# Two attention units per stay of ScalarE's exponential table, with the gates' exponential in the same stay

## The chip, the cores and the metric

The kernel runs on one core of a Trainium2 chip. The core has five instruction streams that run side by side and meet only at semaphores: TensorE (PE in the profile, with its weight loads as PEld), VectorE (DVE), ScalarE (ACT), GpSimd (POOL) and SyncE (SP). Transfers are issued from SP, ACT and POOL queues and carried by 16 DMA engines. Each engine takes its own instructions strictly in the order in which the program lists them, so an instruction that waits holds up everything behind it on its engine.

The metric is the device time of one execution in microseconds. Three executions of the kernel before took 598.86, 600.32 and 600.51 us, median 600.32.

## What is computed

The inputs are 2048 tokens of 512 channels, in float32. Two branches are computed from the same tokens and mixed per token with a gate:

```
g = sigmoid((x * gate_w).sum(-1, keepdims=True))
# A: attention, 32 heads of 16 channels, each query sees 8 keys at distances 0, 2, ..., 14
logits = einsum("bhsd,bhswd->bhsw", q, kg) * 16 ** -0.5     # -1e9 before the first token
a = einsum("bhsw,bhswd->bhsd", softmax(logits), vg) @ wo
# B: gated feed-forward network, hidden width 1792
b = (gelu(x @ w_gate) * (x @ w_up)) @ w_down
return g * a + (1 - g) * b
```

The attention is too small for TensorE's array: eight keys per query. It is computed on VectorE, as elementwise products and reductions. TensorE does the projections and the feed-forward network, with each float32 operand split into a high and a low part (`hi`, `lo`) and three matmuls for a product: high by high, high by low, low by high.

## The kernel before, in words

**Halves, steps, units.** The tokens are worked off in two halves, `par` 0 and 1 (even and odd tokens, so that a distance of 2 is a distance of 1 within a half). For each half, `ffn(par)` runs 14 steps `f`, one for each 128 of the 1792 hidden channels. Between the two, `kq_second` computes keys and queries of the second half. The attention of a half is four **units** (`par`, `u`) of 128 channels, that is 8 heads.

**A step of the feed-forward network** (`gate_up`) makes the gate and up projections as seven block products of a Strassen-like scheme, called a11, s1, s2, a12, s4, s3, a22 after their token operands. Each is six matmuls of 128x512 on line L443 into one of the four PSUM banks `p`. In the profile, token operands show as `A` (a11, a12, a22) or `S` (s1, s2, s3, s4) and the weights as `g`; there are two weight tiles for a step, one with three operands (128x768, for a11, s1, s2) and one with four (128x1024, for the other four). ScalarE and VectorE empty the banks: L523 copies the product of a11 to a second bank, L448 copies twice to `s`, L538 and L554 are the GELUs (`c`), L453 adds, L457 multiplies gate by up, L459 and L460 split the result into `hh` and `hl`. The product a22 of a step is issued in the next step (`fourth`), and its GELU is L554.

**The weights of a step** are built ahead: VectorE forms sums (L382, three instructions a step), ScalarE writes the negated sum into the low part (L400), GpSimd adds the full sum onto it with an accumulating DMA (L401), and ScalarE writes the high part (L405). TensorE can begin a11 of a step only when the L401 transfer of its 128x768 tile has landed. In the second half the three-operand tile comes ready-made from HBM instead. The down projection (L486) runs in the same steps, two steps late; half of its sums are kept in SBUF and put back into a `p` bank by ScalarE before (L480) and taken out after (L502).

**A unit of the attention** is scores, softmax, gate, mix. `scores` is eight VectorE instructions of 2.3 us and a mask (L230). `softmax` is maximum (L237), subtraction (L239), exponential on ScalarE (L241), sum (L245) and reciprocal (L247). `gated` multiplies by the token's gate (L255, L257). `mix` multiplies by the values and adds up (L271 to L284). The gate itself needs one more exponential on ScalarE (L167, `gates`).

**What sets the order.** The program is not written engine by engine. The attention is a Python generator, and `pull` takes pieces of it between the products of a step; `LG`, `m` and the other tiles come from pools with one buffer, `lg` with two. A scheduler then orders each engine's instructions by priority and by when it reckons them ready, so a change at one place shifts rows on all engines for a long way behind it. `paced` ties an instruction to the matmul emitted last, `ordered` fixes the order of two instructions on an engine without a wait, and `after` makes one wait for another.

**ScalarE's tables.** Ahead of an activation whose function is not in the table that is loaded, the compiler puts an ACT_TABLE_LOAD. Plain copies appear behind either table without a load. Exponential (L241, L167) and GELU (L538, L554) do not share one, so each time that ScalarE goes to an exponential and back there are two loads. Such a visit is called a stay here.

Of the kernel before, what the change touches and what calls it, by code (L numbers as in the profile page):

```python
# [10 lines left out]
F32 = mybir.dt.float32  # L11
F32R = mybir.dt.float32r
AF = mybir.ActivationFunctionType
OP = mybir.AluOpType
AX = mybir.AxisListType

P = 128
S, D, F = 2048, 512, 1792
H, DH, W = 32, 16, 8
NT = S // P  # L20
NP = NT // 2
# [9 lines left out]
UH = UC // DH  # L31
# [17 lines left out]
def tile_gated_mix(ctx: ExitStack, tc: tile.TileContext, xt, wqkv, wff, wo, out):  # L49
    nc = tc.nc  # L50
    ctx.enter_context(nc.allow_non_contiguous_dma(reason="rows of 512 bytes"))
    pool = ctx.enter_context(tc.tile_pool(name="sb", bufs=1))
# [67 lines left out]
    z = pool.tile([P, 2, NP], F32, name="z")  # L120
# [42 lines left out]
        if not hh:  # L163
            nc.scalar.activation(z[:, par, jj:jj + 1], ps[:, CU:CU + 1], AF.Copy)

    def gates(par, ex=None):
        first = nc.scalar.activation(en, z[:, par], AF.Exp, scale=-1.0)  # L167
        if ex:
            ordered(first, ex)
        nc.vector.tensor_scalar_add(en, en, 1.0)  # L170
        nc.vector.reciprocal(g[:, par], en)
        nc.vector.tensor_scalar(gc[:, par], g[:, par], -1.0, 1.0, op0=OP.mult, op1=OP.add)
# [10 lines left out]
    LG = {}  # L183
# [8 lines left out]
    def load_kq(par, u):  # L192
        hh, c = divmod(u, 2)
        k, q = slots_of(u > 0), KQ["a"][:, 2 * NP - 1:]
        if u == 1:
            q = pool.tile([P, 2, BT * UC], F32, name="tb").rearrange("p a (b c) -> p (a b) c", c=UC)
        LG[par, u] = k, q
        if not u:
            return
        loads = load_slots(k, KS[par, hh][c])  # L200
        loads.append(nc.sync.dma_start(q, QS[par, hh][c].rearrange("(p j) d -> p j d", j=NP)))
        if not par and u < NU - 1:
            for ins in loads:
                after(ins, SCORED[-1])
# [13 lines left out]
    def scores(par, u):  # L218
# [12 lines left out]
            first, first, mask[:1, None, :NP - 1, :W - 1].to_broadcast([1, UH, NP - 1, W - 1]), op=OP.min)]  # L231
        LG[par, u] = lg

    def softmax(par, u):
        lg = LG[par, u]
        m = pool.tile([P, UH, NP], F32, name="m")
        nc.vector.tensor_reduce(m, lg, axis=AX.X, op=OP.max)  # L237
        yield 0.7
        nc.vector.tensor_tensor(lg, lg, m[:, :, :, None].to_broadcast([P, UH, NP, W]), op=OP.subtract)  # L239
        yield 0.7  # L240
        ex = nc.scalar.activation(lg, lg, AF.Exp, scale=DH ** -0.5)  # L241
        if not (par or u):
            ordered(ex, COPIED[-1])
            gates(par, ex)
        nc.vector.tensor_reduce(m, lg, axis=AX.X, op=OP.add)  # L245
        yield 0.7
        nc.vector.reciprocal(m, m)  # L247
        LG[par, u] = lg, m

    def gated(par, u):  # L250
        lg, m = LG[par, u]
        LG[par, u] = lg
        if par and not u:
            gates(par)
        nc.vector.tensor_tensor(m, m, g[:, par, None, :].to_broadcast([P, UH, NP]), op=OP.mult)  # L255
        yield 0.4
        nc.vector.tensor_tensor(lg, lg, m[:, :, :, None].to_broadcast([P, UH, NP, W]), op=OP.mult)  # L257
        yield 0.7
# [33 lines left out]
    def after(ins, other, cls=mybir.DependencyClass.Sync):  # L292

        tc.add_manual_dep(ins.ins, other.ins.name, mybir.DependencyInfo(cls, mybir.DependencyReason.SCHED_ONLY),
                          reason="pace")
# [4 lines left out]
    def ordered(ins, other):  # L300
        after(ins, other, mybir.DependencyClass.NoSync)

    def need(*key):
        while key not in done:
            yield None

    def attention():
        units = [(0, u) for u in range(NU)] + [(1, u) for u in range(NU)]
        yield from need(0, 0)
        load_kq(0, 0)  # L310
        yield from scores(0, 0)
        load_kq(0, 1)
        yield from scores(0, 1)
        yield from need(0, 1)
        scored, mixed = 2, False
        for i, un in enumerate(units):
            if scored == i:
                yield from need(un[0], un[1] // 2 * 2)
                load_kq(*un)
                if un[1]:  # L320
                    yield LOAD
                else:
                    load_kq(un[0], 1)
                yield from scores(*un)
                scored += 1
                mixed = False
            yield from softmax(*un)
            if un == (1, 0):
                yield from scores(*units[scored])
                scored += 1  # L330
                yield from need(un[0], 1)
            yield from gated(*un)


            to = units[scored] if scored < len(units) else None
            ahead = to and (to[0], to[1] // 2 * 2) in done
            if ahead:
                load_kq(*to)
            yield from mix(*un, LOAD if mixed else 0.0)
            done.add((*un, "o"))  # L340
            mixed = not ahead
            if ahead:
                yield from scores(*to)
                scored += 1

    fill = attention()
    credit = [0.0]

# [114 lines left out]
    late, COPIED = [], []  # L463
# [740 lines left out]
    en = pool.tile([P, NP], F32, name="en")  # L1204
# [51 lines left out]
```

## Time and profile before

| | |
|---|---|
| median of three runs | 600.32 us |
| the profiled execution's own time | 600.41 us |
| its span, first to last instruction | 598.5 us |
| TensorE matmuls busy | 591.7 us, 99% |
| TensorE weight loads busy | 493.0 us, 82% |
| VectorE busy | 529.3 us, 88% |
| ScalarE busy | 391.7 us, 65% |
| GpSimd busy | 89.2 us, 15% |
| ACT_TABLE_LOAD | 20, of 1283 ns each |
| TensorE clock granted | 1.000 |

The profile is of one execution. The 1.9 us between its span and its time lie outside the span. A row such as `L443 PE MATMUL p<-S,g 128*128 128x512 f32 x672 | 167.2, 389 | 0.0` is a group: line, engine, operation, tile written and tiles read, shapes, count, then busy microseconds of all, mean nanoseconds of one, idle microseconds of the engine just ahead of them and what ended that idle time. Durations of matmuls overlap, since they are pipelined, so the distance between starts tells more than their length. In a timeline the first two numbers are start and duration in microseconds, and a bracket at the end gives the idle time ahead of the row and what ended it.

### The profile page before, as it was taken

How to read it: one execution, taken by the hardware profiler on the slowest of the kernel's cores; microseconds unless marked ns; L12 is line 12 of the kernel's file. 1: busy time of each engine (PE TensorE's matmuls, PEld its weight loads, DVE VectorE, ACT ScalarE, POOL GpSimd, SP SyncE). 2: the span in 40 equal slices, each digit the busy share in tenths (PEclk: the TensorE clock that was granted, in tenths of full speed). 3: DMA queues.
4: the chain of work that ended last, by engine and by line, in shares of the span. 5: the costliest groups of instructions: out<-in, count | busy, mean ns of one | idle time of the engine just before them, and what ended most of it. 6: DMA issues, size and time to landing. Idle time of an engine off the chain costs nothing.

```text
span 598.5 us, 8195 instructions
## 1 busy us (share of the span) xinstructions
PE 591.7 (99%) x2778; PEld 493.0 (82%) x2778; DVE 529.3 (88%) x618; ACT 391.7 (65%) x670; POOL 89.2 (15%) x121
## 2 busy tenths in 40 slices
PE   8999999999999999999999999999999999999997
PEld 6889988878788888888788988888888888888886
DVE  5997979998996999799989988999998989799952
ACT  5846558686678767787772465677667656885532
POOL 0501011111111111102017000111111111101300
PEclk9999999999999999999999999999999999999999
DMA  8788897798989988978569948695967696737924
GB/s 312 268 245 249 234 321 199 173 291 220 268 253 237 245 260 231 295 235 328 199 196 317 285 141 281 152 254 125 276 164 229 174 276 159 226 107 193 144 53 156
DMA packets 80449, 134.18 MB, mean 224 GB/s; under 512 B 8092, under 2 KB 46362, under 8 KB 80152
## 3 DMA queue, kind: packets, MB, share of 16 engines
q1 hardware_dynamic: 62890, 97.67, 49.9%
q0 software_dynamic: 12576, 32.97, 28.0%
q10 hardware_dynamic: 4942, 3.01, 1.7%
q8 instruction: 22, 0.36, 0.3%
q14 instruction: 19, 0.16, 0.1%
HBM read 68.30 MB, written 38.86 MB: 179 GB/s over the span
## 4 chain that ended last, share of the span: by engine, by line
PE 90%; DMA 4%; issue 3%; DVE 1%; ACT 1%; SPq 0%; POOL 0%; POOLq 0%; ACTq 0%; DVEq 0%
PE p L443 41%; PE acc L486 11%; PE p L486 11%; PE acc L130 8%; PE acc L771 6%; PE p L771 6%; PE p L704 5%; DMA g<-raw 3%; PE acc L704 2%; DMA prod<-wqkv 1%; DVE g L771 0%; SPq L866 0%; DVE S L771 0%; DVE prod L275 0%; ACT rt L502 0%
## 5 line engine op out<-in xcount | busy, mean ns | idle before, releaser
L443 PE MATMUL p<-S,g 128*128 128x512 f32 x672 | 167.2, 389 | 0.0
L443 PEld LDWEIGHTS p<-S,g 128*128 128x128 f32 x672 | 125.7, 188 | 25.9
L443 PE MATMUL p<-A,g 128*128 128x512 f32 x504 | 128.8, 391 | 0.7 <-DMA g<-raw 0.7
L443 PEld LDWEIGHTS p<-A,g 128*128 128x128 f32 x504 | 93.9, 188 | 22.0 <-DMA g<-raw 1.5
L401 POOL DMA_DIRECT2D g<-raw x40 | 34.6, 865 | 271.1 <-ACT g L400 195.6
L226 DVE TENSOR_REDUCE lg<-prod 128x128 f32<-128x2048 f32 x32 | 72.9, 2278 | 0.1
L486 PE MATMUL p<-d,hh 128*128 128x512 f32 x224 | 68.4, 390 | 0.5 <-ACT p L480 0.5
L486 PE MATMUL acc<-d,hh 128*128 128x512 f32 x224 | 59.0, 390 | 0.0
L271 DVE TENSOR_TENSOR prod<-kq,lg 128x2048 f32<-128x2048 f32 x24 | 54.6, 2274 | 1.0 <-PE acc L486 0.7
L486 PEld LDWEIGHTS p<-d,hh 128*128 128x128 f32 x224 | 41.9, 188 | 9.8 <-ACT p L480 1.2
L486 PEld LDWEIGHTS acc<-d,hh 128*128 128x128 f32 x224 | 42.0, 188 | 8.9
L400 ACT ACTIVATE g<-raw 128x1024 fp32r<-128x1024 f32 (+1 forms) x40 | 39.4, 985 | 12.6 <-DVE raw L382 5.6
L405 ACT ACTIVATE g<-raw 128x1024 fp32r<-128x1024 f32 (+1 forms) x40 | 39.3, 986 | 11.7 <-PE p L443 11.7
L448 ACT ACTIVATE s<-p 128x512 f32<-128x512 f32 x56 | 33.1, 594 | 19.2 <-PE p L443 16.4
L453 DVE TENSOR_TENSOR c<-p,s 128x512 f32<-128x512 f32 x56 | 37.9, 680 | 8.3 <-PE p L443 7.4
L460 DVE TENSOR_TENSOR hl<-c,hh 128x512 fp32r<-128x512 f32 x56 | 38.2, 682 | 7.6 <-ACT hh L459 7.5
L457 DVE TENSOR_TENSOR c<-c 128x512 f32<-128x512 f32 x56 | 38.1, 681 | 6.4 <-ACT c L554 6.3
L459 ACT ACTIVATE hh<-c 128x512 fp32r<-128x512 f32 x56 | 35.1, 626 | 13.2 <-DVE c L457 13.0
L486 PE MATMUL p<-d,hl 128*128 128x512 f32 x112 | 42.4, 389 | 0.0
L502 ACT ACTIVATE rt<-p 128x512 f32<-128x512 f32 x48 | 28.1, 594 | 19.3 <-PE p L486 19.3
L275 DVE TENSOR_TENSOR prod<-prod 128x1024 f32<-128x1024 f32 x32 | 38.9, 1216 | 0.2
L130 PE MATMUL acc<-d,A 128*128 128x256 f32 (+1 forms) x288 | 37.9, 281 | 0.0
(183 smaller groups left out, 982.7 us busy)
## 6 DMA issues: line engine op xcount, KB each, us to landing
g<-raw POOLq DMA_DIRECT2D x27, 512.0 KB, 6.6
raw<-wff SPq DMA_DIRECT2D x42, 256.0 KB, 4.0
ws<-g SPq DMA_DIRECT2D x14, 768.0 KB, 5.8
g<-ws SPq DMA_DIRECT2D x14, 768.0 KB, 5.2
r<-wff SPq DMA_DIRECT2D x28, 256.0 KB, 5.0
d<-r POOLq DMA_DIRECT2D x24, 256.0 KB, 6.7
g<-raw POOLq DMA_DIRECT2D x13, 384.0 KB, 6.3
os<-tb SPq DMA_DIRECT2D x64, 64.0 KB, 3.4
```

The source lines that it names most:

```text
L130: LAST[:] = [nc.tensor.matmul(ps[:, :cn], a[:, t], w[:, c0:c0 + cn], start=(kc == 0 and n == 0), stop=(kc == KC - 1 and n == 2))]
L226: nc.vector.tensor_reduce(two_of(lg, jj), prod.rearrange("p j w (h d) -> p (j w) h d", d=DH), axis=AX.X, op=OP.add)
L271: paced(nc.vector.tensor_tensor(prod.rearrange("p j w (h d) -> p (j w) h d", d=DH), spans(v, jj).rearrange("p j w (h d) -> p j w h d", d=D ...
L275: nc.vector.tensor_tensor(prod[:, :, :4], prod[:, :, :4], prod[:, :, 4:], op=OP.add)
L400: nc.scalar.activation(lo, raw, AF.Copy, scale=-1.0)
L405: ins = nc.scalar.activation(hi, raw, AF.Copy)
L443: LAST[:] = [nc.tensor.matmul(ps, w_, a_, start=(start and kc == 0 and n == 0), stop=(kc == 1 and n == 2), skip_group_check=True)]
L457: nc.vector.tensor_tensor(ge, ge, up, op=OP.mult)
L460: nc.vector.tensor_tensor(hl_, ge, hh_.bitcast(F32), op=OP.subtract)
L486: ins = nc.tensor.matmul(pp, a[:, ts], w, start=(i == 0 and n == 0 and gr == 0), stop=(i == 1 and n == 2), skip_group_check=True)
L704: ins = nc.tensor.matmul(pa, a, b, start=(first and n == 0), stop=(last and n == 2), skip_group_check=True)
L771: return lambda *args, **kw: self.add(getattr(self.eng, name)(*args, **kw))
```

## The change

Before, each unit's softmax had its own exponential, and the gates' exponentials were one beside the first unit's and one by itself in the second half. That makes nine stays and, with the loads at the beginning, twenty table loads. After, `exps` is called at every even unit. It does maximum and subtraction of that unit and of the next, then both exponentials one behind the other; the first waits for the second unit's subtraction. At unit 0 of either half the gates' exponential follows at once. What remains in `softmax` is the sum and the reciprocal. At unit (1, 0) the scores of unit (1, 1) and the wait for the second half's values now stand ahead of the softmax, not inside it. There are four stays and ten table loads.

```diff
-    def gates(par, ex=None):
-        first = nc.scalar.activation(en, z[:, par], AF.Exp, scale=-1.0)
-        if ex:
-            ordered(first, ex)
+    def gates(par, ex):
+        ordered(nc.scalar.activation(en, z[:, par], AF.Exp, scale=-1.0), ex)
...
+    def exps(par, u):
+
+        for lg in (LG[par, u], LG[par, u + 1]):
+            m = pool.tile([P, UH, NP], F32, name="m")
+            nc.vector.tensor_reduce(m, lg, axis=AX.X, op=OP.max)
+            yield 0.7
+            sub = nc.vector.tensor_tensor(lg, lg, m[:, :, :, None].to_broadcast([P, UH, NP, W]), op=OP.subtract)
+            yield 0.7
+        for i in range(2):
+            lg = LG[par, u + i]
+            ex = nc.scalar.activation(lg, lg, AF.Exp, scale=DH ** -0.5)
+            if i:
+                ordered(ex, first)
+                continue
+            first = ex
+            after(ex, sub)
+            if not (par or u):
+                ordered(ex, COPIED[-1])
+        if not u:
+            gates(par, ex)
+
     def softmax(par, u):
+        if u % 2 == 0:
+            yield from exps(par, u)
         lg = LG[par, u]
         m = pool.tile([P, UH, NP], F32, name="m")
-        nc.vector.tensor_reduce(m, lg, axis=AX.X, op=OP.max)
-        yield 0.7
-        nc.vector.tensor_tensor(lg, lg, m[:, :, :, None].to_broadcast([P, UH, NP, W]), op=OP.subtract)
-        yield 0.7
-        ex = nc.scalar.activation(lg, lg, AF.Exp, scale=DH ** -0.5)
-        if not (par or u):
-            ordered(ex, COPIED[-1])
-            gates(par, ex)
         nc.vector.tensor_reduce(m, lg, axis=AX.X, op=OP.add)
...
     def gated(par, u):
...
-        if par and not u:
-            gates(par)
...
-            yield from softmax(*un)
             if un == (1, 0):
                 yield from scores(*units[scored])
                 scored += 1
                 yield from need(un[0], 1)
+            yield from softmax(*un)
             yield from gated(*un)
```

The scheduler's order of all engines differs from the first removed exponential on. In the changed kernel the lines behind the diff's first part lie lower: of those named here, L241 is L242, and the lines from L400 on are 11 higher (L400 is L411, L443 is L454, L523 is L534, L554 is L565), those of `softmax` and `gated` 13 and 11 (L245 is L258, L257 is L268). Three places matter.

**ScalarE, first half, around step 4.** Ahead of the step stood the exponential of unit (0, 0); this is where unit (0, 1)'s stood. L523 is the copy of step 4's a11. Before:

```order
L523 ACTIVATE p<-p 128x512
L459 ACTIVATE hh<-c 128x512
L448 ACTIVATE s<-p 128x512
L429 ACTIVATE d<-r 128x512
L448 ACTIVATE s<-p 128x512
L241 ACT_TABLE_LOAD
L241 ACTIVATE lg<-lg 128x512
L400 ACTIVATE g_1343<-raw 128x768
L405 ACTIVATE g_1343<-raw 128x768
L554 ACT_TABLE_LOAD
L554 ACTIVATE c<-p 128x512
L400 ACTIVATE g_1389<-raw 128x1024
```

After, from the last split ahead of the stay:

```order
L443 ACTIVATE d<-r 128x512
L242 ACT_TABLE_LOAD
L242 ACTIVATE lg<-lg 128x512 x2
L167 ACTIVATE en<-z 128x8
L470 ACTIVATE hh<-c 128x512
L513 ACTIVATE rt<-p 128x512
L534 ACTIVATE p<-p 128x512
L411 ACTIVATE g_1346<-raw 128x768
L565 ACT_TABLE_LOAD
L565 ACTIVATE c<-p 128x512
L411 ACTIVATE g_1393<-raw 128x1024
L491 ACTIVATE p<-rt 128x512
```

The stay with both units' exponentials and the gates' now stands ahead of L523 of step 4. The negated weights of step 5 (`g_1343` before, `g_1346` after) come right behind L523, and the load for the GELU comes behind them.

**TensorE and ScalarE, first half, from step 7 to step 8.** After the change, TensorE's rows between the second part of step 7 (`g_1664`) and a11 of step 8 (`g_1748`). Ahead of these twelve rows and behind a12 of step 7 stand another 9 down-projection matmuls:

```order
L497 MATMUL p<-d,hh 128x512 x2
L454 MATMUL p<-S,g_1664 128x512 x6
L497 MATMUL p<-d,hl 128x512
L454 MATMUL p<-S,g_1664 128x512 x6
L497 MATMUL acc_1071<-d,hl 128x512
L497 MATMUL acc_1072<-d,hl 128x512
L497 MATMUL acc_1073<-d,hl 128x512
L497 MATMUL p<-d,hh 128x512 x2
L497 MATMUL p<-d,hl 128x512
L497 MATMUL p<-d,hh 128x512 x2
L497 MATMUL p<-d,hl 128x512
L454 MATMUL p<-A,g_1748 128x512 x6
```

And ScalarE's rows of the same step, from the copy of a11 to the negated weights of step 8; L549 is the GELU of a12:

```order
L534 ACTIVATE p<-p 128x512
L565 ACTIVATE c<-p 128x512
L470 ACTIVATE hh<-c 128x512
L491 ACTIVATE p<-rt 128x512
L459 ACTIVATE s<-p 128x512 x2
L470 ACTIVATE hh<-c 128x512
L549 ACTIVATE c<-p 128x512
L411 ACTIVATE g_1748<-raw 128x768
L416 ACTIVATE g_1748<-raw 128x768
```

Before, ScalarE's rows of that step were these (`g_1745` are the same weights; L538 is the GELU of a12):

```order
L523 ACTIVATE p<-p 128x512
L459 ACTIVATE hh<-c 128x512
L448 ACTIVATE s<-p 128x512
L554 ACTIVATE c<-p 128x512
L480 ACTIVATE p<-rt 128x512
L400 ACTIVATE g_1745<-raw 128x768
L448 ACTIVATE s<-p 128x512
L538 ACTIVATE c<-p 128x512
L405 ACTIVATE g_1745<-raw 128x768
```

The negated weights of step 8 moved from ahead of the step's second L448 copy to behind the GELU of a12.

**VectorE, first half, last step.** The rows behind the subtraction of unit (0, 3), before:

```order
L453 TENSOR_TENSOR c<-p,s 128x512
L245 TENSOR_REDUCE m<-lg 128x64
L457 TENSOR_TENSOR c<-c 128x512
L247 RECIPROCAL m<-m 128x64
L453 TENSOR_TENSOR c<-p,s 128x512
L255 TENSOR_TENSOR m<-m,g 128x64
L460 TENSOR_TENSOR hl<-c,hh 128x512
L271 TENSOR_TENSOR prod<-kq,lg 128x2048
L257 TENSOR_TENSOR lg<-lg,m 128x512
L771 TENSOR_TENSOR A<-raw,A 128x512 x2
L275 TENSOR_TENSOR prod<-prod 128x2x512
```

and after:

```order
L464 TENSOR_TENSOR c<-p,s 128x512
L258 TENSOR_REDUCE m<-lg 128x64
L468 TENSOR_TENSOR c<-c 128x512
L260 RECIPROCAL m<-m 128x64
L464 TENSOR_TENSOR c<-p,s 128x512
L266 TENSOR_TENSOR m<-m,g 128x64
L268 TENSOR_TENSOR lg<-lg,m 128x512
L471 TENSOR_TENSOR hl<-c,hh 128x512
L282 TENSOR_TENSOR prod<-kq,lg 128x2048
L258 TENSOR_REDUCE m<-lg 128x64
L782 TENSOR_TENSOR A<-raw,A 128x512 x2
L286 TENSOR_TENSOR prod<-prod 128x2x512
```

Sum, reciprocal and the two gate products (L255, L257) of unit (0, 2), whose exponential stood some 65 us earlier, now stand here, and those of unit (0, 3) follow behind the first L271 of the mix.

## The prediction

> **What bounds the kernel now.** I read the page first.
>
> ```profile
> PE 591.7 (99%) x2778; PEld 493.0 (82%) x2778; DVE 529.3 (88%) x618; ACT 391.7 (65%) x670; POOL 89.2 (15%) x121
> PE 90%; DMA 4%; issue 3%; DVE 1%; ACT 1%; SPq 0%; POOL 0%; POOLq 0%; ACTq 0%; DVEq 0%
> ```
>
> TensorE is busy 99% of the span and makes 90% of the chain that ended last; ScalarE, on which the change works, has 1% of that chain. How much TensorE could still gain is told by a view of windows, in which matmuls are counted.
>
> ```profile
> core 0: us, PE busy (x) PEld busy (x) DVE busy (x) ACT busy (x) POOL busy (x), PEclk, DMA share, GB/s
> 164.00:270.00 106.00, 106.00 (x468) 87.48 (x467) 96.62 (x116) 81.16 (x129) 16.29 (x19) 1.00 0.90 252
> 350.00:540.00 190.00, 190.00 (x846) 157.41 (x845) 175.25 (x188) 132.24 (x208) 21.71 (x26) 1.00 0.74 198
> ```
>
> ```profile
> 186.69 1.28 ACT L241 ACT_TABLE_LOAD   x1
> 511.36 1.28 ACT L241 ACT_TABLE_LOAD   x1
> ```
>
> 106 us / 468 is 226.5 ns a matmul, and 190 us / 846 is 224.6 ns (the matmuls at the edges count whole). So 227 ns is the rate without gaps, and nearly 300 us of the program run at it. Seven of the nine stays lie in these two windows (the loads that begin the first and the last of the seven are shown) and cost TensorE next to nothing. Loads as such are therefore not the price; what counts is where a stay meets something that TensorE waits for. That is around 123 us, at the stay of unit (0, 1). TensorE's timeline there:
>
> ```profile
> 130.64 0.73 PE L486 MATMUL p<-d,hh 128*128 128x512 f32 x2
> 131.21 0.39 PE L486 MATMUL p<-d,hl 128*128 128x512 f32 x1
> 132.11 0.73 PE L486 MATMUL p<-d,hh 128*128 128x512 f32 x2 [0.50 <-ACT p L480]
> 132.67 0.40 PE L486 MATMUL p<-d,hl 128*128 128x512 f32 x1
> 132.91 0.63 PE L443 MATMUL p<-A,g 128*128 128x512 f32 x2
> 134.01 1.20 PE L443 MATMUL p<-A,g 128*128 128x512 f32 x4 [0.47 <-DMA g<-raw]
> 135.04 1.08 PE L486 MATMUL p<-d,hh 128*128 128x512 f32 x4
> ```
>
> From 130.64 to 135.04 twelve matmuls start in 4.40 us; at 227 ns they need 2.72. So 1.7 us are lost, first to L480, then to the L401 transfer of step 5's weights. Both stand behind the stay on ScalarE:
>
> ```profile
> 123.36 1.28 ACT L241 ACT_TABLE_LOAD   x1
> 124.65 0.63 ACT L241 ACTIVATE lg<-lg 128x512 f32<-128x512 f32 x1
> 125.19 0.83 ACT L400 ACTIVATE g<-raw 128x768 fp32r<-128x768 f32 x1
> ...
> 126.77 1.28 ACT L554 ACT_TABLE_LOAD   x1
> ...
> 129.51 0.59 ACT L538 ACTIVATE c<-p 128x512 f32<-128x512 f32 x1
> 129.99 0.60 ACT L480 ACTIVATE p<-rt 128x512 f32<-128x512 f32 x1
> ...
> 131.46 0.60 ACT L480 ACTIVATE p<-rt 128x512 f32<-128x512 f32 x1
> ```
>
> Without load, exponential and load (1.28 + 0.54 + 1.28 = 3.1 us by starts) the second L480 would have ended by about 129 and L400 begun 1.8 us sooner, more than the stalls behind them. The other losses after the head are small: the chain of waits and the weight loads' own timeline name them.
>
> ```profile
> 126.31 7.65 DMA g<-raw
> 147.19 9.04 DMA g<-raw
> 103.26 0.77 PEld L443 LDWEIGHTS p<-A,g 128*128 128x128 f32 x4 [0.40 <-DVE c L453]
> 156.27 0.30 PEld L443 LDWEIGHTS p<-A,g 128*128 128x128 f32 x2 [0.63 <-DMA g<-raw]
> 286.07 0.53 PEld L771 LDWEIGHTS p<-g,A 128*128 128x128 f32 x3 [0.69 <-ACT p L771]
> PEld p L443 <- DVE c L453: 1.0, 3, 0.4
> ```
>
> In every gap-free stretch a weight load of 0.19 us is followed by 0.04 us of idle, so these brackets overstate by that: 0.6 at 156, about 0.4 at 103, 0.65 at 286, and some 0.6 in the other two L453 waits.
>
> The Trainium skill, Perfetto Trace Analysis, section Identifying the Most-Contended Engine, says that matmul busy time misleads and that the busy share of LDWEIGHTS tells how near TensorE is to its limit. By it 18% would be free. Here the trace differs: the windows without any gap show 87.48/106 = 83%, so 82% over the span is full.
>
> **The change, part by part.** The sum is made against the profiled execution, 600.41 us (span 598.5, 1.9 outside), which stands 0.1 above the median of 600.32.
>
> *Ten loads fewer, nine stays to four.*
>
> ```profile
> DVE m L245 <- ACT lg L241: 8.0, 6, 2.7
> ```
>
> 10 x 1.28 = 12.8 us of ScalarE go. By the windows that is worth nothing outside the stay at 123, and there 1.7 us, if nothing equal takes its place. VectorE waited 8.0 us in six sums for exponentials; with four waits at most 2.7 us each it may save some, but it waits for TensorE often enough that I count nothing.
>
> *The joint stay of units (0, 0) and (0, 1).* ScalarE's new order puts it ahead of L523 of step 4, behind L432.
>
> ```profile
> 115.88 0.63 ACT L432 ACTIVATE d<-r 128x512 fp32r<-128x512 f32 x1 [1.21 <-PE p L443]
> 117.72 1.52 PE L443 MATMUL p<-A,g 128*128 128x512 f32 x6
> ```
>
> With the times of before it would run from 116.5 for 1.28 + 0.54 + 0.54 + 0.2 = 2.6 us, and L459, L502 and L523 (0.5 us each by starts) would end near 120.8. TensorE's new order has a11 from 117.72 and 30 matmuls (6.8 us) before s2, which needs L523: 124.5. That covers it by 3.7 us. Step 5's L400 comes right behind, at about 121, not 125.19; its sums (L382) now stand behind VectorE's wait for these exponentials, which may make it 122. L480 comes two L400, a load and a GELU behind, near 126; TensorE comes to it 45 matmuls behind 117.72, at 127.9. So I put the new stay at 0; if the cover were gone it would cost what the old one did, 1.7. The moved L400 is why I count the 1.7 as won. The weights of step 6 move forward the same way (their L400 stands right behind the GELU of a22 now), which takes the 0.6 at 156 with it; I count 0.5. Where unit (0, 0)'s stay stood (94.5) there is none now, and half of the 0.4 at 103 is counted, 0.2, its bounds being 0 and 0.4.
>
> *Later weights in step 8.* L400 of step 8 now stands behind the GELU of a12 in step 7. From the last matmul of a12 to a11 of step 8 TensorE has 33 matmuls, 33 x 0.227 + 0.2 = 7.7 us to the start. ScalarE and GpSimd need 0.4 (that matmul's length), 0.5 (the GELU, by starts), 1.1 (125.19 to 126.31, L400 to its transfer's issue), and the landing:
>
> ```profile
> g<-raw POOLq DMA_DIRECT2D x13, 384.0 KB, 6.3
> DMA to landing us min/median/max: 3.8/6.4/9.9
> ```
>
> 2.0 + 6.3 = 8.3 us, so 0.6 are lost. With the shortest landing it is 0, with the longest 2.0 + 9.9 - 7.7 = 4.2. I take 0.6, the median's.
>
> *VectorE at the end of the first half.*
>
> ```profile
> 254.18 0.69 DVE L245 TENSOR_REDUCE m<-lg 128x64 f32<-128x512 f32 x1 [0.64 <-ACT lg L241]
> 255.38 0.55 DVE L247 RECIPROCAL m<-m 128x64 f32<-128x64 f32 x1
> 256.39 0.21 DVE L255 TENSOR_TENSOR m<-m,g 128x64 f32<-128x64 f32 x1
> ...
> 259.46 0.68 DVE L257 TENSOR_TENSOR lg<-lg,m 128x512 f32<-128x512 f32 x1
> ...
> 275.85 0.69 DVE L460 TENSOR_TENSOR hl<-c,hh 128x512 fp32r<-128x512 f32 x1 [0.70 <-ACT hh L459]
> 277.23 2.29 DVE L271 TENSOR_TENSOR prod<-kq,lg 128x2048 f32<-128x2048 f32 x1 [0.69 <-PE acc L486]
> ```
>
> Four more instructions come here, 0.69 + 0.55 + 0.21 + 0.68, less 0.08 of overlap each: 1.8 us. VectorE is without idle time from 254 except for 0.70 + 0.69 = 1.4, so 0.4 stay over and delay the sums that ScalarE's copies ahead of 286 wait for. I add 0.4; bounds 0 and 1.8.
>
> *The end.* The last instructions of the mix may run later too, by at most the 1.8.
>
> ```profile
> 585.37 0.69 DVE L88 TENSOR_TENSOR hl<-raw,hh 128x512 fp32r<-128x512 f32 x1 [6.44 <-ACT hh L87]
> 589.38 0.62 PE L704 MATMUL p<-S,hh 128*128 128x512 f32 x2
> ```
>
> The last split ends at 586.1; TensorE's last group, the earliest user of it, begins at 589.4 at the soonest. 3.3 us of cover less 1.8 less the 1.4 won leave 0.1: no cost, but no reserve either. The added `after` on the first exponential waits for a subtraction that VectorE does early (115 against 117.8 by the rows moved), so it queues nothing; the moved softmax of (1, 0) has its mix behind the same scores as before.
>
> Sum: 600.4 - 1.7 - 0.5 - 0.2 + 0.6 + 0.4 = 599.0 us.
>
> **The rivals.**
>
> *Every gap in the first half goes.* For it speaks that all of them hang on ScalarE or VectorE, which are relieved; against it, the L453 waits at 196 and 270 lie far from any stay. It gives 1.7 + 0.6 + 0.4 + 0.6 less, 597.1.
>
> *The lead is lost again before the second half.* If VectorE reaches 254 as late as before, the 2.4 us won ahead of it end as a longer wait at 286: 600.4 with the 0.4 left out. For it: VectorE has only 1.4 us of idle in the 23 to 277. Against it: the row at 254 was released by an exponential, and the idle at 277 by TensorE, so both move ahead with them. It decides where TensorE comes to these rows first.
>
> *Step 8 waits for its weights.* This is the slower end. For it speaks the landing of 9.04 us above, of the larger tile of step 6; against it, the median of 6.3. With 9.9 us the term is 4.2, not 0.6: 602.6. It turns the sum from gain to loss at a landing above 7.7 us (0.6 + 1.4 = 2.0 lost).
>
> *TensorE has room after all*, as the 82% would have it: then the 12.8 us of ScalarE would count, 587.6. The gap-free windows speak against it.
>
> **How the numbers follow.** Chances: forecast 0.41, all gaps gone 0.19, lead lost 0.16, step 8 late 0.23, room 0.01. The forecast is that of the likeliest, 599.0. A difference of 0.3%, 1.8 us, is about what a measurement of this kernel can tell from none; 599.0 and 600.4 lie within it of 600.32, 597.1 and 587.6 below, 602.6 above: faster 0.20, same 0.57, slower 0.23. The range reaches most of the way to the two outer cases, 597.3 to 602.6; the forecast's own, by bounds of its small terms, is 598.0 to 600.4.
>
> **What would show it.** Ten loads of 1283 ns; no wait of L486 for L480 near 130; L400 of step 5 ahead of 122 and its transfer landed before a11; 468 matmuls or so in 106 us in the undisturbed stretch; a weight-load wait for `g<-raw` of about 0.6 us at a11 of step 8, some 178 to 180 us in; a wait at 284 to 286 of 1.0 us, not 0.65. I am wrong if new waits of TensorE appear where the order moved and I saw cover, above all behind the stay at 117, or if the sum of TensorE's gaps changes by more than 2 us either way.

## The result: 0.55% slower

The changed kernel takes 603.31 us (median of 8 runs, 602.07 to 606.13), the kernel before 600.13 us (median of 8, 598.86 to 600.51): a ratio of 1.0055, 95% interval 1.0044 to 1.0067. The forecast was 599.0, with a range of 597.3 to 602.6; the time lies above it. The profiled execution of the changed kernel took 602.94 us, with a span of 600.7, 2.2 longer than the span before.

From the page of the changed kernel, the busy times and the table loads:

```profile
PE 590.9 (98%) x2778; PEld 493.1 (82%) x2778; DVE 531.3 (88%) x618; ACT 380.2 (63%) x660; POOL 89.2 (15%) x121
L242 ACT ACT_TABLE_LOAD x4 | 5.1, 1283 | 0.1
L565 ACT ACT_TABLE_LOAD x4 | 5.1, 1283 | 0.1
L782 ACT ACT_TABLE_LOAD x1 | 1.3, 1283 | 1.7 <-PEq L1259 1.7
L549 ACT ACT_TABLE_LOAD x1 | 1.3, 1283 | 0.4 <-ACT hl L160 0.4
```

The change does what it says: ten loads are left of twenty, and ScalarE is busy 11.5 us less. TensorE's matmuls and weight loads are as many as before and as long within 0.8 us in all. What differs is when TensorE waits. Both kernels have 2778 matmuls, so the start of one after, less the start of the one with the same number before, tells at every point how far ahead (minus) or behind (plus) TensorE is. The numbers count from 0. The points where that changes:

| matmul | before, us | after, us | difference |
|---|---|---|---|
| 535 | 103.61 | 103.04 | -0.56 |
| 662 | 134.01 | 131.83 | -2.18 |
| 758 | 156.27 | 153.59 | -2.68 |
| 936 | 196.87 | 193.94 | -2.93 |
| 1075 | 228.55 | 226.25 | -2.30 |
| 1260 | 270.55 | 269.99 | -0.56 |
| 1320 | 284.29 | 285.13 | +0.84 |
| 1326 | 286.07 | 287.56 | +1.49 |
| 1772 | 366.75 | 368.86 | +2.11 |
| last | 594.60 | 596.84 | +2.25 |

So TensorE leads by 2.9 us in the first half, and five places between 226 and 369 us give back 5.0. These are two single executions, though. 0.3 us of the lead is there at 25 us (matmul 100), far ahead of the first changed row, and the five kernels below that are ordered as before up to there, but for an issue or two at 54 us (third, seventh to tenth run), stand 0.3 to 0.9 us ahead of this same profile at matmul 936. What the change wins in the first half is therefore 2.0 to 2.6 us. The profile of the changed kernel also is one of its quicker executions: the medians are 3.2 us apart, the two spans 2.2.

The weight loads' timeline of the changed kernel names what each of the five waited for (bracket: idle time ahead, and what ended it):

```profile
226.25 0.99 PEld L497 LDWEIGHTS acc<-d,hh 128*128 128x128 f32 x5 [1.07 <-DMA d<-r]
269.99 1.23 PEld L454 LDWEIGHTS p<-A,g 128*128 128x128 f32 x6 [1.73 <-DVE c L464]
285.13 1.24 PEld L782 LDWEIGHTS acc<-g,A 128*128 128x128 f32 x6 [1.66 <-ACT c L508]
287.56 1.00 PEld L782 LDWEIGHTS p<-g,A 128*128 128x128 f32 x5 [1.19 <-ACT p L782]
368.86 2.15 PEld L454 LDWEIGHTS p<-A,g 128*128 128x128 f32 x10 [0.88 <-DMA g<-raw]
```

**What was won.** ScalarE's timeline at the new joint stay, and TensorE's where the two stalls of before stood:

```profile
115.91 1.28 ACT L242 ACT_TABLE_LOAD   x1
117.20 1.15 ACT L242 ACTIVATE lg<-lg 128x512 f32<-128x512 f32 x2
...
120.89 0.85 ACT L411 ACTIVATE g<-raw 128x768 fp32r<-128x768 f32 x1 [0.95 <-DVE raw L393]
```

```profile
131.38 0.61 PE L497 MATMUL p<-d,hh 128*128 128x512 f32 x2
...
132.74 2.88 PE L454 MATMUL p<-A,g 128*128 128x512 f32 x12
135.46 0.84 PE L454 MATMUL p<-S,g 128*128 128x512 f32 x3
```

The stay costs TensorE nothing, step 5's negated weights are written at 120.89, and from 131.38 to 135.46 eighteen matmuls start in 4.08 us, 0.227 us each. This is where 1.7 us were lost before.

**Where the largest part went.** These are TensorE's last down-projection products of the first half (L486 before, L497 after; 273 to 281 us) in the kernel before, and in the changed kernel:

```profile
276.58 1.07 PE L486 MATMUL acc<-d,hl 128*128 128x512 f32 x4
277.49 1.98 PE L486 MATMUL p<-d,hh 128*128 128x512 f32 x8
...
280.21 5.60 PE L771 MATMUL acc<-g,A 128*128 128x512 f32 x24
```

```profile
276.02 1.98 PE L497 MATMUL p<-d,hh 128*128 128x512 f32 x8
277.84 1.07 PE L497 MATMUL acc<-d,hl 128*128 128x512 f32 x4
...
279.65 4.24 PE L782 MATMUL acc<-g,A 128*128 128x512 f32 x18
```

The scheduler has turned two pieces round: the four `acc<-d,hl`, which finish the four accumulators, stand behind eight `p<-d,hh`. The second half's first products (`acc<-g,A`, 24 of them) need those accumulators' banks, and ScalarE must store them first. ScalarE's timeline in the kernel before, and in the changed kernel:

```profile
277.01 0.69 ACT L497 ACTIVATE s<-acc,gc 128x512 f32<-128x512 f32 x1 [1.19 <-PE acc L486]
...
281.96 0.71 ACT L497 ACTIVATE c<-acc,gc 128x512 f32<-128x512 f32 x1
282.53 1.30 ACT L497 ACTIVATE rt<-p,gc 128x512 f32<-128x512 f32 x2
```

```profile
278.26 0.69 ACT L508 ACTIVATE s<-acc,gc 128x512 f32<-128x512 f32 x1 [3.52 <-PE acc L497]
...
282.07 2.43 ACT L508 ACTIVATE rt<-p,gc 128x512 f32<-128x512 f32 x4
284.35 0.72 ACT L508 ACTIVATE c<-acc,gc 128x512 f32<-128x512 f32 x1
```

The stores (L497 before, L508 after) begin at 278.26, before at 277.01, although TensorE is still ahead at 270. The fourth store stands behind all four of the other banks' (`rt<-p`) and ends at 285.07, at which TensorE's last six of 24 begin. Before, that bank was free at 282.67 and all 24 ran without a gap.

### The profile page after: what moved, and what is told of

Same layout as the page of the kernel before. It is cut to its first block, busy times and chain, and to the rows that moved or that the text cites. A ratio compares the mean times of both kernels' runs of the same rounds, so it can differ in the third digit from the quotient of the medians.

```text
span 600.7 us, 8191 instructions
## 1 busy us (share of the span) xinstructions
PE 590.9 (98%) x2778; PEld 493.1 (82%) x2778; DVE 531.3 (88%) x618; ACT 380.2 (63%) x660; POOL 89.2 (15%) x121
## 4 chain that ended last, share of the span: by engine, by line
PE 89%; DMA 5%; issue 3%; ACT 1%; DVE 1%; SPq 0%; POOL 0%; POOLq 0%; ACTq 0%
PE p L454 40%; PE p L497 11%; PE acc L497 11%; PE acc L130 8%; PE acc L782 7%; PE p L782 5%; PE p L715 5%; DMA g<-raw 2%; PE acc L715 2%; DMA d<-r 2%; DMA ws<-g 1%; DMA raw<-xt 1%; ACT rt L508 0%; DVE prod L282 0%; ACT c L508 0%
## 5 line engine op out<-in xcount | busy, mean ns | idle before, releaser
L454 PE MATMUL p<-S,g 128*128 128x512 f32 x672 | 165.7, 389 | 0.0
L454 PEld LDWEIGHTS p<-S,g 128*128 128x128 f32 x672 | 125.6, 188 | 25.8
L454 PE MATMUL p<-A,g 128*128 128x512 f32 x504 | 126.8, 390 | 1.8 <-DVE c L464 1.3
L454 PEld LDWEIGHTS p<-A,g 128*128 128x128 f32 x504 | 94.2, 188 | 22.2 <-DVE c L464 1.7
L497 PE MATMUL p<-d,hh 128*128 128x512 f32 x224 | 68.6, 390 | 0.0
L497 PE MATMUL acc<-d,hh 128*128 128x512 f32 x224 | 59.0, 390 | 0.6 <-DMA d<-r 0.6
L497 PEld LDWEIGHTS acc<-d,hh 128*128 128x128 f32 x224 | 42.0, 188 | 9.8 <-DMA d<-r 1.1
L497 PEld LDWEIGHTS p<-d,hh 128*128 128x128 f32 x224 | 42.0, 188 | 9.0 <-ACT p L491 0.3
L411 ACT ACTIVATE g<-raw 128x1024 fp32r<-128x1024 f32 (+1 forms) x40 | 39.4, 985 | 10.4 <-DMA ks<-hl 4.5
L464 DVE TENSOR_TENSOR c<-p,s 128x512 f32<-128x512 f32 x56 | 37.9, 684 | 8.3 <-PE p L454 7.4
L470 ACT ACTIVATE hh<-c 128x512 fp32r<-128x512 f32 x56 | 35.0, 626 | 12.2 <-DVE c L468 11.7
L497 PE MATMUL p<-d,hl 128*128 128x512 f32 x112 | 42.6, 389 | 0.0
L221 DVE TENSOR_TENSOR prod<-v,kq 128x2048 f32<-128x2048 f32 x16 | 36.5, 2278 | 2.4 <-PE p L454 2.3
```

What stands on the lines that cost most here:

```text
L411: nc.scalar.activation(lo, raw, AF.Copy, scale=-1.0)
L454: LAST[:] = [nc.tensor.matmul(ps, w_, a_, start=(start and kc == 0 and n == 0), stop=(kc == 1 and n == 2), skip_group_check=True)]
L497: ins = nc.tensor.matmul(pp, a[:, ts], w, start=(i == 0 and n == 0 and gr == 0), stop=(i == 1 and n == 2), skip_group_check=True)
```

## Experiments

Theory A, formed on this comparison: what is lost belongs to the order that the scheduler gives the turn to the second half, which units (0, 2) and (0, 3) bring about, and to transfers that come no sooner for a TensorE that is ahead. Theory B (and V, its version for one wait): VectorE is late, by the four instructions that it has more to do at 250 to 263 us, as the prediction had it. Theory C: any change of the order costs about as much, wherever it is. All ratios are to the kernel before.

### One part of the change at a time

The first three and the eighth run make only some of the pairs share a stay. `JOINT` lists them; all other units do their softmax as before. Where (1, 0) is not listed, the second half's gates and unit (1, 1)'s scores stay where they were before.

```diff
+    JOINT = ((0, 2),)
+
     def softmax(par, u):
-        if u % 2 == 0:
+        if (par, u) in JOINT:
             yield from exps(par, u)
         lg = LG[par, u]
         m = pool.tile([P, UH, NP], F32, name="m")
+        if (par, u // 2 * 2) not in JOINT:
+            nc.vector.tensor_reduce(m, lg, axis=AX.X, op=OP.max)
...
+            ex = nc.scalar.activation(lg, lg, AF.Exp, scale=DH ** -0.5)
```

> Only units (0, 2) and (0, 3) share a stay; everything else, the second half too, is as before. Theory A (the loss is made at the turn to the second half, where this pair's stay moves the last group of down's products: the four matmuls acc<-d,hl now stand behind eight p<-d,hh, and the fourth store of an accumulator behind the four stores rt<-p): no lead is won in the first half, the matmuls of 226 and 270 wait no more than before, and the first products of the second half lose 1.5 to 2.3 us at 285 to 288; time 601.5 to 602.5. Theory B (VectorE's four more instructions at 250 to 263 are late): the loss comes earlier, at 266 to 272, as a wait of TensorE for L464's sums of c, 1 to 2 us; time also 601 to 602.5. Theory C (any change of the order costs about a microsecond, wherever it is): some 601, with losses at places that differ from those of the changed kernel.

Measured: 604.27 us, ratio 1.0059 (1.0044 to 1.0074). This one pair makes the kernel slower by as much as the whole change does. Its weight-load rows with a wait, from 225 us on:

```profile
259.65 1.00 PEld L511 LDWEIGHTS acc<-d,hh 128*128 128x128 f32 x5 [2.25 <-DMA d<-r]
286.79 1.23 PEld L796 LDWEIGHTS acc<-g,A 128*128 128x128 f32 x6 [1.66 <-ACT c L522]
289.23 0.99 PEld L796 LDWEIGHTS p<-g,A 128*128 128x128 f32 x5 [1.21 <-ACT p L796]
```

The two waits at the turn are the changed kernel's, to the hundredth in the first; there is none for L464's sums (L478 here), against theory B. A wait of 2.0 us for the down weights at 259.65 was expected by neither, and the time lies above what either expected.

With `JOINT = ((0, 0),)`:

> Only units (0, 0) and (0, 1) share a stay, with the gates of the first half in it; all else as before, and the last group of down's products has its accumulators first, as before. Theory A: TensorE is 2.2 to 2.9 us ahead by 220, loses 1 to 1.5 of it at 264 to 270, where the second transfer raw<-xt lands no sooner than before, and nothing more at 285; time 598.5 to 599.8. Theory B: the same up to 250, then no wait at 270 either, since VectorE has no more to do there than before: 597.5 to 598. Theory C: some 601.

Measured: 598.40 us, ratio 0.9970 (0.9959 to 0.9981). It is 0.3% faster than the kernel before, and the fastest of all. The time lies just below A's range and above B's. TensorE is 2.2 us ahead at 132, 3.0 at 194, and still 2.5 at 283.6. ScalarE's stores at the turn in this kernel, and TensorE's wait behind the transfer `raw<-xt`, for a bank that ScalarE fills:

```profile
274.25 0.69 ACT L522 ACTIVATE s<-acc,gc 128x512 f32<-128x512 f32 x1 [0.58 <-PE acc L511]
...
278.06 0.69 ACT L522 ACTIVATE c<-acc,gc 128x512 f32<-128x512 f32 x1
278.63 2.44 ACT L522 ACTIVATE rt<-p,gc 128x512 f32<-128x512 f32 x4
```

```profile
268.44 0.30 PEld L511 LDWEIGHTS p<-d,hh 128*128 128x128 f32 x2 [0.69 <-ACT p L505]
```

The accumulators come first, in both engines. The wait at 268 is there, but of 0.5 us and not the 1 to 1.5 that A had put on it: the transfer alone does not make the 1.5 of the changed kernel.

With `JOINT = ((1, 0), (1, 2))`, and the second half's gates as in the changed kernel:

> Only the four units of the second half share two stays, with its gates in the first of them; the first half is as before. All theories but C: the six loads of tables that go in the second half lie in a stretch without gaps and give nothing; the wait of 0.6 at 369 for the weights g<-raw is there or not: 600.1 to 600.8. Theory C: some 601.

Measured: 600.27 us, ratio 1.0001 (0.9991 to 1.0012). Six loads fewer in the second half are worth nothing. With `JOINT = ((1, 2),)`:

> Only units (1, 2) and (1, 3) share a stay; the rest is as before. Both stays lie in stretches where TensorE has no gap, before and after. Theory A: nothing gained, nothing lost: 599.9 to 600.6. Theory C (any change of the order costs about a microsecond): some 601.

Measured: 600.44 us, ratio 1.0008 (0.9999 to 1.0017). Theory C falls with these two: they move some 200 of TensorE's rows each, and neither kernel is 0.3% off.

### The order of the last group

The fourth run lays down two orders in the changed kernel (`ordered` sets an order and no wait):

```diff
+                if gr == NG - 1 and not par:
+                    if b and i == 1 and n == 0:
+                        ordered(ins, MK["mm"])
+                    elif not b:
+                        MK["mm"] = ins
                 LAST[:] = [ins]
...
-            nc.scalar.activation(st, pp, AF.Copy, scale=gc[:, par, jj:jj + 1])
+            act = nc.scalar.activation(st, pp, AF.Copy, scale=gc[:, par, jj:jj + 1])
+            if b:
+                ordered(act, MK["st"])
+            else:
+                MK["st"] = act
```

> The changed kernel with two orders laid down for the last group of down's products: the matmuls acc<-d,hl ahead of the p<-d,hh of the second product of each p, and the fourth store of an accumulator ahead of the stores rt<-p, as in the kernel before. Nothing else moves. Theory A: the 1.5 us at 285 and about half of the 0.9 at 287 come back, the 1.5 at 270 stays: 601.0 to 602.0. Theory B: VectorE is late all the same, the wait moves to another instruction and the time stays within 0.5 of 603.3.

Measured: 600.75 us, ratio 1.0005 (0.9994 to 1.0015). Twelve matmuls and five stores in another order take 2.6 us off the changed kernel's median, more than A expected; in the profile the wait at 285 is gone and 1.9 us are back by 286. Nothing else on TensorE, VectorE or ScalarE changed places between these two kernels. So this order is what makes the changed kernel slower than the one before: with it mended they take the same time. The reverse is the sharper test. The ninth run puts the changed kernel's order of this group into the kernel before, in which nothing of the softmax is touched:

```diff
+                if gr == NG - 1 and not par and i == 1:
+                    if not b and n == 2:
+                        MK.setdefault("hl", []).append(ins)
+                    if b and t == BT - 1 and n == 1:
+                        for x in MK["hl"]:
+                            ordered(x, ins)
...
+            act = nc.scalar.activation(st, pp, AF.Copy, scale=gc[:, par, jj:jj + 1])
+            if jj == BT - 1:
+                MK["st"] = act
+            if b:
+                ordered(MK["st"], act)
```

> The kernel before, with every stay as it was, and only the order of the changed kernel laid down in the last group of down's products: the four matmuls acc<-d,hl behind the eight p<-d,hh (TensorE), the fourth store of an accumulator (c<-acc,gc) behind all four rt<-p (ScalarE). Theory A (the order alone is the price): ScalarE's stores begin 8 x 0.227 = 1.8 us later, the fourth accumulator is free at about 286 and not at 282.7, so the first products of the second half wait about 1.8 us at 284 and the copies behind them some 0.5 more than before: 602.0 to 602.8. If instead the loss needs the late VectorE or the late transfers of the changed kernel: within 0.5 us of the kernel before.

Measured: 601.83 us, ratio 1.0024 (1.0013 to 1.0034); 1.5 us, a little under what A expected. By the profiles TensorE loses 1.8 us between matmuls 1314 and 1326 that it does not lose before; the fourth run got back 1.8 us between the same two. ScalarE's stores and the weight loads in this kernel:

```profile
278.31 0.69 ACT L504 ACTIVATE s<-acc,gc 128x512 f32<-128x512 f32 x1 [2.99 <-PE acc L487]
...
282.11 2.42 ACT L504 ACTIVATE rt<-p,gc 128x512 f32<-128x512 f32 x4
284.39 0.72 ACT L504 ACTIVATE c<-acc,gc 128x512 f32<-128x512 f32 x1
```

```profile
285.17 1.23 PEld L782 LDWEIGHTS acc<-g,A 128*128 128x128 f32 x6 [1.66 <-ACT c L504]
287.37 1.00 PEld L782 LDWEIGHTS p<-g,A 128*128 128x128 f32 x5 [0.98 <-ACT p L782]
```

The stores are the changed kernel's within 0.05 us, and so is the first wait; the second is 0.98 for 1.19. They come from the order alone. The tenth run has only the last of the diff's two parts, the place of the fourth store:

> The kernel before with the smaller half of that order: only the store c<-acc,gc of the fourth accumulator behind all four rt<-p on ScalarE, TensorE's order as before. The store begins 1.1 us later and ends near 284; the product that writes that bank again began at about 284.3. Theory A: nothing or up to 0.3 us lost, the matmuls' order is what costs: 600.0 to 600.5. If the store's place is the cause: 601 or more.

Measured: 600.18 us, ratio 0.9995 (0.9986 to 1.0004). So the store's place alone costs nothing, and TensorE's order is needed for the loss; whether that order costs as much without the store's, no run shows. The eleventh run has the first experiment's one pair, with the order of the group laid down as in the fourth:

> Only units (0, 2) and (0, 3) share a stay, as in the first run, and the order of the last group of down's products is laid down as in the kernel before. Theory A: the 1.4 at 286.8 and half of the 0.95 at 289 go, the wait of 2.0 for the down weights d<-r at 259.7 stays if it belongs to the order of this kernel (it went unforeseen there): 601.4 to 602.2. If that wait was only one run's: 599.9 to 600.6.

Measured: 602.23 us, ratio 1.0030 (1.0017 to 1.0043): 2.0 us less than without the mend, at the upper end of what A expected. The wait for the down weights is there again, in a second kernel with the same order up to there, so it is not one execution's accident:

```profile
260.62 0.99 PEld L512 LDWEIGHTS acc<-d,hh 128*128 128x128 f32 x5 [1.81 <-DMA d<-r]
```

### The wait at 270

Changed kernel, ScalarE and then VectorE ahead of the wait, from the first sum of unit (0, 2) on:

```profile
264.17 0.63 ACT L782 ACTIVATE A<-raw 128x512 fp32r<-128x512 f32 x1 [2.47 <-DMA raw<-xt]
```

```profile
251.06 0.69 DVE L258 TENSOR_REDUCE m<-lg 128x64 f32<-128x512 f32 x1 [0.58 <-ACT lg L242]
...
264.84 0.69 DVE L782 TENSOR_TENSOR A<-raw,A 128x512 fp32r<-128x512 f32 x1 [1.61 <-ACT A L782]
265.84 0.69 DVE L782 TENSOR_TENSOR A<-raw,A 128x512 fp32r<-128x512 f32 x1 [0.31 <-ACT A L782]
266.45 2.28 DVE L282 TENSOR_TENSOR prod<-kq,lg 128x2048 f32<-128x2048 f32 x1
268.66 1.28 DVE L464 TENSOR_TENSOR c<-p,s 128x512 f32<-128x512 f32 x2
```

In the kernel before, VectorE had the same rows in another order:

```profile
264.67 2.28 DVE L271 TENSOR_TENSOR prod<-kq,lg 128x2048 f32<-128x2048 f32 x1
266.87 1.29 DVE L771 TENSOR_TENSOR A<-raw,A 128x512 fp32r<-128x512 f32 x2
...
269.21 1.28 DVE L453 TENSOR_TENSOR c<-p,s 128x512 f32<-128x512 f32 x2
```

VectorE is not late: it waits 1.9 us for splits that ScalarE cannot begin until `raw<-xt` has landed, at 264.1 here; in the kernel before it landed at 263.0 and held nobody up. The load went out no sooner than before, at 257.54 for 257.59, since by the profile it waits for two transfers that read its buffer, `g<-raw` and `ws<-raw`. These were issued 1.2 and 1.95 us sooner, but took 8.4 and 11.7 us for 7.4 and 6.3, and landed at 257.3 and 257.5. Then comes a product of 2.28 us of the mix, which stood ahead of the splits before, and only then the sums for TensorE. Two runs, both with the last group's order mended as in the fourth, test that. The fifth moves the product:

```diff
-            paced(nc.vector.tensor_tensor(prod.rearrange("p j w (h d) -> p (j w) h d", d=DH),
+            ins = (nc.vector.tensor_tensor(prod.rearrange("p j w (h d) -> p (j w) h d", d=DH),
...
+            paced(ins)
+            if (par, u, jj) == (0, 2, 2):
+                MK["prod"] = ins
...
+        if k == 1 and n == "a11" and "prod" in MK:
+            ordered(ins, MK["prod"])
```

> The kernel of the run before it (changed kernel, order of the last group laid down), and one more order laid down on VectorE: the second product prod<-kq,lg of unit (0, 2)'s mix (L282, 2.28 us, at 266.45 in the changed kernel) stands ahead of the two splits A<-raw that wait for the second transfer raw<-xt, not behind them. With it the two sums L464 come directly behind the splits. Theory A: the wait of 1.47 at 270 is made by this product, which stands between the transfer's landing at 264.2 and the sums; with it gone the sums are done 1 to 2 us sooner, the wait falls to 0.5 or less, and the time to 599.3 to 600.0, if the rest keeps its lead. Theory V: VectorE is late by the sum, reciprocal and two products of unit (0, 2) that it does at 251 to 254 (2.1 us); then the product is late too, the splits begin later, and the wait stays above 1.0: 600.4 to 601.

Measured: 603.00 us, ratio 1.0053 (1.0037 to 1.0070); slower than without it, where A expected 599.3 to 600.0. The runs lie from 601.65 to 604.87, and the profiled one, with 601.84, is one of the quickest. VectorE, and a later row of ScalarE:

```profile
265.72 1.28 DVE L795 TENSOR_TENSOR A<-raw,A 128x512 fp32r<-128x512 f32 x2
266.92 0.68 DVE L467 TENSOR_TENSOR c<-p,s 128x512 f32<-128x512 f32 x1
```

```profile
282.00 2.42 ACT L517 ACTIVATE rt<-p,gc 128x512 f32<-128x512 f32 x4 [2.45 <-PE p L501]
```

The part about 270 came about as expected: the sums begin 1.7 us sooner and TensorE's wait there falls from 1.5 to 0.7 us. The second run agrees: there too ScalarE waits 2.48 us for `raw<-xt`, the product stands ahead of the splits, and TensorE loses 0.5. But the scheduler answered by moving eight `p<-d,hh` of the last group in between the second half's first products, so the stores of those banks wait until 282.0 and TensorE loses 2.2 us at 286.0. The sixth run makes VectorE's extra work small. It leaves out most of the sum, the reciprocal and the two gate products of unit (0, 2):

```diff
+        n = 1 if (par, u) == (0, 2) else UH
+        q = 1 if (par, u) == (0, 2) else NP
-        nc.vector.tensor_reduce(m, lg, axis=AX.X, op=OP.add)
+        nc.vector.tensor_reduce(m[:, :n, :q], lg[:, :n, :q], axis=AX.X, op=OP.add)
```

and the same for the reciprocal and the two products of `gated`.

> The changed kernel with the order of the last group laid down, and with the sum, the reciprocal, the gate's factor and the normalisation of unit (0, 2) done for one element instead of all (L258, L260, L266, L268: the rest of that unit's softmax is left out). VectorE has some 1.5 to 2 us less to do at 251 to 254; its rows around 265 to 270 keep their order, but for a neighbour or two. Theory A: VectorE comes to the splits A<-raw sooner and waits longer there for raw<-xt, the sums L464 come when they came, and the wait at 270 stays at 1.2 to 1.5: 600.4 to 601.0. Theory V: the wait at 270 shrinks by 1 us or more: 599.3 to 599.9.

Measured: 600.84 us, ratio 1.0016 (1.0005 to 1.0026); the fourth run, which has that work, took 600.75. VectorE in this kernel, and the wait:

```profile
265.38 0.69 DVE L796 TENSOR_TENSOR A<-raw,A 128x512 fp32r<-128x512 f32 x1 [2.74 <-ACT A L796]
...
269.20 1.28 DVE L468 TENSOR_TENSOR c<-p,s 128x512 f32<-128x512 f32 x2
```

```profile
270.53 1.23 PEld L458 LDWEIGHTS p<-A,g 128*128 128x128 f32 x6 [1.70 <-DVE c L468]
```

VectorE is done 0.5 us sooner than in the fourth run and waits longer for the transfer (2.74 us for 1.58; 0.65 of it because `raw<-xt` landed that much later), and TensorE's wait is the same (1.72 there). Theory V falls.

### The second half's gates

The seventh run moves only the second half's gate exponential behind unit (1, 0)'s, with its scores and waits, and leaves all units their own stays:

```diff
             if not (par or u):
                 ordered(ex, COPIED[-1])
+            if not u:
                 gates(par, ex)
...
-        if par and not u:
-            gates(par)
```

> Only the second half's gates: their exponential (L167) stands right behind unit (1, 0)'s, with unit (1, 1)'s scores and the wait for the values ahead of it, as in the changed kernel; every unit keeps its own stay. One stay of ScalarE less, the one that began at 350.54 before. If the wait of 0.6 at 367 to 369 belongs to this part: that wait is there, g<-raw of step 2 lands 11 us behind its issue and not 9.9, and the time is 600.3 to 601.0. If it belongs to the pairs: no wait, 599.9 to 600.4.

Measured: 600.65 us, ratio 1.0013 (1.0004 to 1.0022), and no wait near 367. The time lies where it was expected with that wait (600.3 to 601.0), but the wait is not there; where these 0.1% come from is open. The wait is in all five kernels that have the changed second half (the changed one, third to sixth run, 0.5 to 0.7 us each); in the six others whose second half is as before up to that point TensorE loses more than 0.15 there once, in the eighth run:

```profile
366.83 2.15 PEld L468 LDWEIGHTS p<-A,g 128*128 128x128 f32 x10 [0.86 <-DMA g<-raw]
```

So it goes with the pair (1, 0) and (1, 1), not with the gates alone, but can be there without it; what brings it is open. The third run, which has it, is no slower by its median; what it costs in the changed kernel is not settled beyond "at most 0.6".

## Why the prediction was wrong

**The step that failed** is "VectorE at the end of the first half", +0.4 with bounds of 0 and 1.8. It looked at the right stretch, 250 to 287 us, and at the wrong thing. It priced four VectorE instructions and let the sums wait for them. Their time is worth nothing there: with most of it left out (sixth run), TensorE's wait and the kernel's time stay the same. In its place stand two other losses, 3.8 us in the table from 1075 to 1326: 2.1 at 285 and 287, and 1.7 from 266 to 270. The first is the turned order of the last group, shown from both sides (by the medians, 1.5 us put into the kernel before and 2.6 taken out of the changed one), and without it the changed kernel is no slower than the one before. The rows that show the turn were to be had from the order of the two kernels without any run; the prediction followed VectorE's rows and did not read TensorE's at that place. The second is the transfer that lands no sooner and the product between it and the sums: with the product moved, about 0.8 of the 1.5 us went (fifth run), though a larger loss came elsewhere.

**Stall at 130 to 135, -1.7; weights of step 6, -0.5; wait at 103, -0.2.** Right. In all five kernels with that stay (the changed one, second, fourth to sixth run) TensorE gains 1.6 us on the profile before from matmul 535 to 662, 0.5 from there to 758, and 0.25 up to 535. The kernels whose order is as before up to there gain 0.1 to 0.5, -0.2 to 0.4, and nothing at these places, so the first two terms are rather 1.4 and 0.3; in sum 2.0 to 2.6, where 2.4 was forecast. The new stay at 115.91 hides as worked out (the forecast put it at 116.5), and the moved weights of step 5 are written at 120.89, ahead of 122.

**Step 8's later weights, +0.6.** The weights come later, as said, and nothing waits. The transfer took 4.6 us, not the median of 6.3, and TensorE's a11 began at 176.94 without a wait:

```profile
g<-raw POOLq DMA_DIRECT2D x1, 384.0 KB, 4.6
```

The rival on the slower side hung on this transfer, so the time came out in its direction for none of its reasons.

**Loads in stretches without gaps cost nothing.** Right: third and eighth run, and the windows of the changed kernel:

```profile
164.00:220.00 56.00, 56.00 (x248) 46.37 (x247) 53.00 (x63) 39.83 (x65) 10.27 (x12) 1.00 0.89 249
350.00:540.00 190.00, 189.54 (x848) 157.04 (x848) 174.42 (x185) 124.75 (x201) 21.70 (x26) 1.00 0.73 197
```

TensorE is busy all 56 us of the first with 248 matmuls, one in 0.226 us; the second holds 848 where 846 were before, with 7.5 us less of ScalarE. That also settles the rival in which TensorE had room: six loads less (third run) moved nothing. The Trainium skill (Perfetto Trace Analysis, Identifying the Most-Contended Engine) reads TensorE's headroom from the busy share of weight loads. This trace shows no such headroom: the share is 82% again, and in 56 us without a gap it is 46.37/56 = 83%.

**The lead is lost before the second half.** As a rival this had 0.16 and came closest, but by another mechanism: VectorE came to the first sum behind the last stay at 251.06, 3.1 us ahead of before, not as late. What took the lead were places where TensorE, now ahead, met things that did not come sooner, and then the turned order took more than the lead.

**Not counted at all.** The wait at 226 for down weights (0.6 us of the lead; in the two kernels with the pair (0, 2) and (0, 3) alone, 1.6 to 2.0 at 260) and the one at 369. The clause "I am wrong if new waits of TensorE appear where the order moved and I saw cover, or if the sum of its gaps changes by more than 2 us" is what happened: +2.25. The forecast's own bounds were drawn too tight as well: 598.0 to 600.4 leaves out those of the wait at 103 and of step 8's slow end.

The parts add up roughly: -0.30% for the first pair, +0.59% for the second, +0.01% for the second half make +0.30%, against +0.55% measured. The sum is rough, since the second pair alone pays 2.0 us at 260 that the changed kernel does not pay. The changed kernel in turn has the wait at 270, which the second pair alone does not have; that it meets only a TensorE that is ahead is argued from where it appears.

## What to carry to other kernels

Where a scheduler writes the order, an edit is priced by reading the new order at every place where TensorE changes from one stage to the next, not only where the edited instructions stand: there a dozen matmuls in another order, none of them slower, cost 1.5 to 2.6 us, about what the one useful merged stay had won. Merge what stands in front of a wait and leave the rest: one pair of units in one stay, of four, gave 0.3%, the second took it back and more. And a lead won early lasts only until TensorE meets a transfer that does not land sooner with it, so look for that transfer, and for what it waits for, before counting the lead to the end.

## What the runs showed of the hardware beside

The same accumulating transfers took longer in the kernels in which two loads were issued just ahead of the first of them. In the kernel before, SyncE issued the loads `kq<-vs` (448 and 512 KB) at 215.24 and 216.44, behind GpSimd's first `g<-raw` at 214.19. In the changed kernel they went out at 210.88 and 211.30, ahead of it (212.08). From issue to landing GpSimd's three transfers (`g<-raw` of 384 and 512 KB, `d<-r` of 256 KB) took 7.2, 9.4 and 9.4 us before, and 9.6, 11.1 and 10.7 after. The last is the one that TensorE waits for at 226. With the order of before at this place (second run) they took 7.3, 9.6 and 9.6, and nothing waited; with that of the changed kernel (sixth run) 10.2, 11.4 and 11.1. In all six kernels with the loads first (the changed one, first, fourth to sixth and eleventh run) the first of the three took 9.1 to 10.2 us, in the seven others 7.2 to 8.2. That the loads are the cause is argued from this; no run moved them alone, and the six are also those in which units (0, 2) and (0, 3) share a stay.
